# Turning a strided copy out of PSUM around, and shifting attention steps by one slot, in a fused attention and gated feed-forward kernel

## Chip, cores, metric

One core of one Trainium2 chip. The metric is device time in microseconds (us); every kernel was run several times and medians are quoted. One run of each is profiled, and its "span" (first to last instruction) is 1 to 2 us shorter than the time. Engines are named as in the profile: PE is TensorE (PEld its weight loads), ACT is ScalarE, DVE is VectorE, POOL is GpSimd, SP is SyncE. One scrambling of q and k by the copy, applied to the reference, moves its output by under 1%. The output check is a weak test of this copy; that the changed copy puts every element in its place is read from the code.

## The reference

```
q, k, v: 4 batches x 8 heads x 768 positions x 64, float32
k_sum = max of k over blocks of 32;  v_sum = mean of v over blocks of 32
scores = [ q k^T/8 where |i-j| < 16 ,  q k_sum^T/8 + log 32 ]
attn   = softmax(scores) [v ; v_sum]                       # x: 3072 x 512
out    = x + sigmoid(x w_res) * ((gelu(x w_gate) * (x w_val)) w_out)   # d_ff = 1536
```

## The kernel before

The work is cut into eight units: half a batch each, 384 rows of x. The code fixes the order of the instructions on each engine. A unit has a stage A (twelve steps of gate and value matmuls, gelu, product) and a stage B (six output steps, two per 128 rows). Work for later units is hung into slots: in stage A the transposes of the next batch's k (even units) or q (odd units), in stage B the next unit's attention. Six of the eight units carry transposes; unit 6 has attention work but no transposes; unit 7 has neither.

```python
def transpose_pair(src, dst, pad, hp, pool, tag, copy):     # hp: pair of heads
    tp = pool.tile([128, PJ, PP], BF16, ...)                # PSUM, PJ = 8, PP = 96
    for j in range(PJ):
        for hh in range(2):
            nc.tensor.transpose(tp[hh*64:hh*64+64, j, :], src[:, 2*hp+hh, j, :], ident[0:PP, 0:PP])
    o = dst[:, pad:pad + S].rearrange("d (p j) -> d j p", j=PJ)   # position = 8 p + j
    if copy == "act":
        nc.scalar.copy(o, tp[:])
    else:
        nc.vector.tensor_copy(o, tp[:])
```

```python
# stage A: slots in the feed-forward loop
at(("A", 3 * hp + 1), lambda hp=hp: k_step(nb, hp, ps_t, "t"))      # even units; q_step in odd ones
# stage B: slots in the output loop
for hp in range(NP):
    at(("B", hp), lambda hp=hp: s_step(u + 1, hp, nst))             # scores, exp, mask -> P
    at(("B", hp + 1), lambda hp=hp: av_step(u + 1, hp, nst))        # P v -> xn
at(("B", 4), lambda: xt_step(u + 1, 0, nst, ps_t, "t"))             # transpose of xn -> xT
at(("B", 5), lambda: xt_step(u + 1, 1, nst, ps_t, "t"))
for fo in range(FO):
    fo_step(st, gvT, fo)            # g, vv: 8 matmuls; gelu on ACT; product on DVE
    for fn in slots.get(("A", fo), []): fn()
for i in range(2 * NSUB):
    for fn in slots.get(("B", i), []): fn()
    out_step(u, st, gvT, i // 2, i % 2)   # even: r, f(0-3), tanh; odd: f(4-11), th and o on DVE
```

The softmax here doesn't subtract the row's maximum and nothing guards it: scores larger than these inputs give would overflow.

Of the kernel before, what the change touches and what calls it, by code (L numbers as in the profile page):

```python
# [15 lines left out]
def kernel(  # L16
# [11 lines left out]
    nc = tc.nc  # L28
    B, H, S, D = q.shape
# [13 lines left out]
    NSUB = TU // 128  # L43
# [4 lines left out]
    PJ = 8  # L48
# [11 lines left out]
    ps_t = ctx.enter_context(tc.tile_pool(name="ps_t", bufs=1, space=bass.MemoryType.PSUM))  # L60
# [17 lines left out]
    def load_qk(src, b, parts, name):  # L78
        t = qk.tile([PP, H, PJ, D], BF16, tag=name, name=name)
        hs = H // parts  # L80
        for i in range(parts):
            nc.gpsimd.dma_start(
                out=t[:, i * hs:(i + 1) * hs].rearrange("p h j d -> p h (j d)"),
                in_=src[b, i * hs:(i + 1) * hs].rearrange("h (p j) d -> p h (j d)", j=PJ),
            )
        return t
# [9 lines left out]
    with tc.manual_schedule():  # L96
# [66 lines left out]
        def transpose_pair(src, dst, pad, hp, pool, tag, copy):  # L163
            tp = pool.tile([128, PJ, PP], BF16, tag=tag, name="tp")
            for j in range(PJ):
                for hh in range(2):
                    nc.tensor.transpose(tp[hh * 64:hh * 64 + 64, j, :], src[:, 2 * hp + hh, j, :],  # L167
                                        ident[0:PP, 0:PP])
            o = dst[:, pad:pad + S].rearrange("d (p j) -> d j p", j=PJ)
            if copy == "act":  # L170
                nc.scalar.copy(o, tp[:])  # L171
            else:
                nc.vector.tensor_copy(o, tp[:])

        def k_step(b, hp, pool, tag, copy="act"):
            transpose_pair(k_sb[b], kT[b % 2][hp], WIN, hp, pool, tag, copy)
# [20 lines left out]
        def s_step(u, hp, st):  # L197
            b, half = u // 2, u % 2
            s = ps_s.tile([128, 2, 512], F32, tag="s", name="s")
            kt, qt = kT[b % 2][hp], qT[b % 2][hp]  # L200
            for t in range(HT):
                tt = half * HT + t
                for hh in range(2):
                    ps = slice(hh * 64, hh * 64 + 64)
                    nc.tensor.matmul(s[:, hh, t * QT:(t + 1) * QT], kt[ps, tt * QT:tt * QT + 128],
                                     qt[ps, tt * QT:(tt + 1) * QT], start=True, stop=True,
                                     skip_group_check=True)
            for hh in range(2):
                ps = slice(hh * 64, hh * 64 + 64)
                nc.tensor.matmul(s[96:128, hh, 0:TU], ksum[b % 2][hp][ps, :],  # L210
                                 qt[ps, half * TU:(half + 1) * TU], start=True, stop=True,
                                 skip_group_check=True)
            P = work.tile([128, 2, HT, QT], BF16, tag="P", name="P")
            nc.scalar.activation(P.rearrange("p a t q -> p a (t q)"), s[:, :, 0:TU], AF.Exp,  # L214
                                 scale=scale, bias=bias_t[:])
            Pf = P.rearrange("p a t q -> p (a t) q")
            nc.vector.tensor_mul(Pf, Pf, maskt.unsqueeze(1).to_broadcast([128, 2 * HT, QT]))  # L217
            st["P", hp] = P

        def av_step(u, hp, st):  # L220
            b, half = u // 2, u % 2
            P = st["P", hp]
            ao = ps_o.tile([128, NSUB, 2, D + 1], F32, tag="ao", name="ao")
            for sub in range(NSUB):
                for hh in range(2):
                    for e in range(2):
                        t = 2 * sub + e
                        nc.tensor.matmul(ao[64 * e:64 * e + 64, sub, hh, :], P[:, hh, t, :],  # L228
                                         vext[b % 2][:, half * HT + t, 2 * hp + hh, :],
                                         start=True, stop=True, skip_group_check=True)  # L230
            rz = work.tile([128, NSUB, 2, 1], F32, tag="rz", name="rz")
            nc.vector.reciprocal(rz[:], ao[:, :, :, D:D + 1])
            xn = st["xn"].rearrange("p s (h d) -> p s h d", d=D)[:, :, 2 * hp:2 * hp + 2, :]
            nc.vector.tensor_mul(xn, ao[:, :, :, 0:D], rz.to_broadcast([128, NSUB, 2, D]))  # L234

        def xt_step(u, g, st, pool, tag):
            xp = pool.tile([128, 2, TU], BF16, tag=tag, name="xp")
            for i in range(2):
                ko = 2 * g + i
                for sub in range(NSUB):  # L240
                    nc.tensor.transpose(xp[:, i, sub * 128:(sub + 1) * 128],
                                        st["xn"][:, sub, ko * 128:(ko + 1) * 128], ident[:])
            nc.vector.tensor_copy(st["xT"][:, 2 * g:2 * g + 2, :], xp[:])
# [20 lines left out]
        def out_step(u, st, gvT, sub, part):  # L264
            ss = slice(sub * 128, (sub + 1) * 128)
            if part == 0:
                r = ps_mm.tile([128, 512], F32, tag="mm", name="r")
                for ko in range(KO):
                    nc.tensor.matmul(r[:], st["xT"][:, ko, ss], w_res[:, ko, :],  # L269
                                     start=(ko == 0), stop=(ko == KO - 1))  # L270
                th = work.tile([128, DM], F32, tag="th", name="th")
                nc.scalar.activation(th[:], r[:], AF.Tanh, scale=0.5)  # L272
                f = ps_mm.tile([128, 512], F32, tag="mm", name="f")
                for fo in range(4):
                    nc.tensor.matmul(f[:], gvT[:, fo, ss], w_out[:, fo, :],  # L275
                                     start=(fo == 0), stop=False)
                st["f"], st["th"] = f, th
            else:
                f, th = st["f"], st["th"]
                for fo in range(4, FO):  # L280
                    nc.tensor.matmul(f[:], gvT[:, fo, ss], w_out[:, fo, :],  # L281
                                     start=False, stop=(fo == FO - 1))
                nc.vector.scalar_tensor_tensor(th[:], th[:], 1.0, f[:], ALU.add, ALU.mult)  # L283
                o = work.tile([128, DM], F32, tag="o", name="o")
                nc.vector.scalar_tensor_tensor(o[:], th[:], 0.5, st["xn"][:, sub, :], ALU.mult, ALU.add)
                row = u * TU + sub * 128
                nc.sync.dma_start(out=out[row:row + 128, :], in_=o[:])
# [30 lines left out]
        for u in range(NU):  # L318
            b, half = u // 2, u % 2
            nb = b + 1  # L320
            if half == 0 and nb < B:
                k_sb[nb] = load_qk(k, nb, 1, "k_sb")
                q_sb[nb] = load_qk(q, nb, 1, "q_sb")
                v_loads(nb)
            slots = {}

            def at(key, fn):
                slots.setdefault(key, []).append(fn)

            if nb < B:  # L330
                for hp in range(NP):
                    if half == 0:
                        at(("A", 3 * hp + 1), lambda hp=hp: k_step(nb, hp, ps_t, "t"))
                    else:
                        at(("A", 3 * hp + 1), lambda hp=hp: q_step(nb, hp, ps_t, "t"))
                if half == 1:
                    at(("A", 6), lambda: vsum_mm(nb, ps_t, "t"))
                    at(("A", 6), lambda: vsum_bc(nb, 0, 4, nc.gpsimd))
                    at(("A", 6), lambda: vsum_bc(nb, 4, 8, nc.gpsimd))
                    at(("A", 6), lambda: vsum_bc(nb, 8, NT, nc.gpsimd))  # L340
            nst = None
            if u + 1 < NU:
                nst = new_unit()
                for hp in range(NP):
                    at(("B", hp), lambda hp=hp: s_step(u + 1, hp, nst))
                    at(("B", hp + 1), lambda hp=hp: av_step(u + 1, hp, nst))
                at(("B", 4), lambda: xt_step(u + 1, 0, nst, ps_t, "t"))
                at(("B", 5), lambda: xt_step(u + 1, 1, nst, ps_t, "t"))
            gvT = upool.tile([128, FO, TU], BF16, tag="gvT", name="gvT")
            for fo in range(FO):  # L350
                fo_step(st, gvT, fo)
                for fn in slots.get(("A", fo), []):
                    fn()
            for i in range(2 * NSUB):
                for fn in slots.get(("B", i), []):
                    fn()
                out_step(u, st, gvT, i // 2, i % 2)
            st = nst


# [28 lines left out]
```

## Time and profile before

| | before |
|---|---|
| time | 383.67 us (382.7 to 385.25, 3 runs) |
| span of the profiled run | 381.9 us |
| first g matmul | 54.1 us |
| units with transposes (six) | 42.1 to 45.8 us each |
| unit 6, no transposes | 31.4 us |
| unit 7, no next unit | 30.8 us |

The first line of the page has each engine's busy time, with its share of the span and its number of instructions:

```profile
PE 295.3 (77%) x2640; PEld 155.7 (41%) x2640; DVE 166.1 (44%) x324; ACT 212.1 (56%) x202; POOL 70.9 (19%) x88
```

No engine is full, so averages do not name the bottleneck. Cutting the span at the first g of each unit does. This is the view of busy time by window: start:end, length, then busy us and instructions of each engine, granted TensorE clock, DMA share, GB/s.

```profile
99.93:144.50 44.57, 37.81 (x337) 19.48 (x336) 17.21 (x33) 27.04 (x25) 16.13 (x17) 0.96 1.15 80
144.50:186.60 42.10, 34.10 (x325) 17.94 (x324) 19.87 (x36) 27.01 (x25) 0.00 (x0) 1.00 0.05 20
319.67:351.09 31.42, 30.88 (x262) 16.72 (x261) 16.71 (x32) 13.73 (x21) 0.00 (x0) 1.00 0.07 26
...
```

These are unit 1 (with q), unit 2 (with k) and unit 6 (no transposes). ACT is busy 27 us against 13.7. Four copies make that difference, as the groups by line and form show (the column before the bar is the count; after it busy us and mean ns of one):

```profile
L171 ACT COPY kT_1_94<-tp 128x768 bf16<-128x768 bf16 x2 | 7.2, 3578 | 2.2 <-PE tp L167 2.2
L173 DVE COPY qT_3_100<-tp 128x768 bf16<-128x768 bf16 x1 | 3.6, 3557 | 0.0
L214 ACT ACTIVATE P<-s,bias_t 128x768 bf16<-128x768 f32 x32 | 28.8, 900 | 45.0 <-PE s L210 44.9
```

A copy of 128x768 takes four times as long as an exp of 128x768. What that does at the end of stage A is in the timeline of unit 1 (start, duration, instruction; in brackets the idle time before it and its releaser):

```profile
123.36 3.58 ACT L171 COPY qT_3_104<-tp 128x768 bf16<-128x768 bf16 x1 [0.62 <-PE tp L167]
...
126.44 0.83 ACT L261 ACTIVATE ge<-g 128x384 f32<-128x384 f32 x1
127.28 1.28 ACT L214 ACT_TABLE_LOAD   x1
...
128.58 0.90 ACT L214 ACTIVATE P<-s,bias_t 128x768 bf16<-128x768 f32 x1
...
129.51 0.56 DVE L217 TENSOR_TENSOR P<-P,maskt 128x768 bf16<-128x768 bf16 x1 [1.66 <-ACT P L214]
...
130.12 0.38 PE L228 MATMUL ao<-vext_114,P 128*64 128x65 bf16 x12 [3.02 <-DVE P L217]
...
130.99 3.11 PE L281 MATMUL f<-w_out,gvT 128*128 128x512 bf16 x8
```

Copy, delayed last gelu, table load, exp, mask, and PE idle for 3.02 us. After it the eight f matmuls need 3.11 us in place of 1.9: the clock had been halved for most of them (the mean granted clock from 130.99 to 134.03 is 0.59; in unit 0, whose eight f matmuls take 3.59 us, it is 0.50). The waits (who waited for whom: us in total, times, longest) give the totals:

```profile
PE ao L228 <- DVE P L217: 18.4, 7, 3.0
PE g L254 <- ACT ge L261: 18.0, 14, 1.3
```

### The profile page before, as it was taken

To read this page: it belongs to the slowest core of one execution; us is meant where nothing else is said; L and a number is where in the kernel's file an instruction comes from. 1 tells how busy PE (TensorE), PEld (TensorE's weight loads), DVE (VectorE), ACT (ScalarE), POOL (GpSimd) and SP (SyncE) were. 2 spreads that over 40 slices of the span, in tenths; PEclk is the share of its full clock that TensorE was granted. 3 is DMA by queue.
4 is the path that set the end of the run, shared out by engine and by line. 5 is a ranking of instruction groups with operands and counts; after the bars stand their busy time and mean duration, and the time that the engine had idled before them with its cause. 6 is when DMAs were issued, how large, how long until landed. Compare 5 with 4: busy or idle time off the path is not lost.

```text
span 381.9 us, 6251 instructions
## 1 busy us (share of the span) xinstructions
PE 295.3 (77%) x2640; PEld 155.7 (41%) x2640; DVE 166.1 (44%) x324; ACT 212.1 (56%) x202; POOL 70.9 (19%) x88
## 2 busy tenths in 40 slices
PE   0421668669978698878978698777988699999995
PEld 0320244334544244434544344433554345645652
DVE  4044863434522264335523263435622256456432
ACT  0699317773476745785485736685376833353420
POOL 8523364000008530000007530000004100000000
PEclk9999969987999899999999899998999989999999
DMA  8999999900100991000100994000100001000002
GB/s 156 205 193 197 200 152 121 23 0 30 57 0 6 189 130 47 2 1 29 57 0 2 177 130 64 0 3 8 50 27 2 0 29 57 0 21 36 29 1 82
DMA packets 54843, 23.95 MB, mean 63 GB/s; under 512 B 37408, under 2 KB 51744, under 8 KB 54816
## 3 DMA queue, kind: packets, MB, share of 16 engines
q0 software_dynamic: 42208, 14.98, 51.6%
q1 hardware_dynamic: 8032, 7.44, 6.9%
q10 hardware_dynamic: 4576, 1.15, 1.4%
q8 instruction: 20, 0.33, 0.4%
q14 instruction: 7, 0.06, 0.0%
HBM read 32.24 MB, written 6.29 MB: 101 GB/s over the span
## 4 chain that ended last, share of the span: by engine, by line
PE 49%; ACT 24%; issue 13%; DVE 10%; ACTq 2%; DMA 1%; DVEq 0%
PE f L281 13%; PE vv L258 10%; PE g L254 8%; PE vs L188 3%; PE tp L167 3%; ACT ge L261 3%; PE r L269 2%; PE ao L228 2%; ACT L214 2%; ACTq L105 2%; PE f L275 2%; DVE P L217 2%; ACT kT_1_94 L171 2%; ACT kT_0_93 L171 2%; ACT qT_1_102 L171 2%
## 5 line engine op out<-in xcount | busy, mean ns | idle before, releaser
L254 PE MATMUL g<-xT,w_gate 128*128 128x384 bf16 x384 | 79.0, 328 | 19.3 <-ACT ge L261 18.0
L261 ACT ACTIVATE ge<-g 128x384 f32<-128x384 f32 x96 | 53.0, 573 | 60.9 <-PE g L254 46.3
L262 DVE TENSOR_TENSOR gvT<-ge,vv 128x384 bf16<-128x384 f32 x96 | 51.4, 551 | 78.3 <-ACT ge L261 45.3
L258 PE MATMUL vv<-xT,w_val 128*128 128x384 bf16 x384 | 78.6, 328 | 2.9 <-DVE gvT L262 2.9
L254 PEld LDWEIGHTS <-w_gate 128*128 128x128 bf16 x384 | 35.4, 98 | 47.2 <-issue 24.7
L214 ACT ACTIVATE P<-s,bias_t 128x768 bf16<-128x768 f32 x32 | 28.8, 900 | 45.0 <-PE s L210 44.9
L281 PE MATMUL f<-w_out,gvT 128*128 128x512 bf16 x192 | 52.4, 422 | 0.0
L258 PEld LDWEIGHTS <-w_val 128*128 128x128 bf16 x384 | 37.7, 98 | 29.7 <-issue 5.6
L195 POOL COPY vext_114<-vsum_116 32x2048 bf16<-32x2048 bf16 x6 | 11.1, 1894 | 117.0 <-DVE vsum_116 L190 117.0
L217 DVE TENSOR_TENSOR P<-P,maskt 128x768 bf16<-128x768 bf16 x32 | 20.1, 632 | 20.6 <-ACT P L214 20.5
L281 PEld LDWEIGHTS <-gvT 128*128 128x128 bf16 x192 | 18.8, 106 | 24.8 <-issue 10.3
L283 DVE SCALAR_TENSOR_TENSOR th<-th,f 128x512 f32<-128x512 f32 x24 | 16.5, 688 | 27.2 <-PE f L281 27.2
L272 ACT ACTIVATE th<-r 128x512 f32<-128x512 f32 x24 | 14.3, 594 | 25.0 <-PE r L269 24.6
L228 PEld LDWEIGHTS <-P 128*64 128x64 bf16 x384 | 9.5, 118 | 39.0 <-DVE P L217 28.9
L269 PE MATMUL r<-w_res,xT 128*128 128x512 bf16 x96 | 24.8, 381 | 0.0
L275 PE MATMUL f<-w_out,gvT 128*128 128x512 bf16 x96 | 24.6, 379 | 0.0
L195 POOL COPY vext_113<-vsum_115 32x2048 bf16<-32x2048 bf16 (+1 forms) x4 | 9.1, 2303 | 74.4 <-DVE vsum_115 L190 74.4
L292 POOL DMA_DIRECT2D vext_114<-in_v_dram x24 | 18.2, 761 | 12.9 <-DMA k_sb<-in_k_dram 5.9
L167 PE MATMUL tp<-ident,k_sb 96*64 96x96 bf16 x256 | 9.8, 227 | 12.2 <-DMA k_sb<-in_k_dram 9.6
L228 PE MATMUL ao<-vext_113,P 128*64 128x65 bf16 x192 | 6.9, 214 | 15.0 <-DVE P L217 9.0
L234 DVE TENSOR_TENSOR xn<-ao,rz 128x384 bf16<-128x384 f32 x32 | 17.8, 558 | 1.1
L167 PE MATMUL tp<-ident,q_sb 96*64 96x96 bf16 x256 | 9.8, 227 | 10.0 <-DMA q_sb<-in_q_dram 4.9
(139 smaller groups left out, 338.4 us busy)
## 6 DMA issues: line engine op xcount, KB each, us to landing
out_dram<-o SPq DMA_DIRECT2D x24, 256.0 KB, 2.0
k_sb<-in_k_dram POOLq DMA_DIRECT2D x3, 768.0 KB, 7.5
q_sb<-in_q_dram POOLq DMA_DIRECT2D x3, 768.0 KB, 10.7
vext_114<-in_v_dram POOLq DMA_DIRECT2D x20, 96.0 KB, 10.5
w_gate<-in_moe_w_gate_dram POOLq DMA_DIRECT2D x6, 256.0 KB, 14.8
w_val<-in_moe_w_val_dram POOLq DMA_DIRECT2D x6, 256.0 KB, 14.5
w_out<-in_moe_w_out_dram POOLq DMA_DIRECT2D x3, 512.0 KB, 14.0
vst<-in_v_dram ACTq DMA_DIRECT2D x5, 192.0 KB, 11.1
```

What stands on the lines that cost most here:

```text
L167: nc.tensor.transpose(tp[hh * 64:hh * 64 + 64, j, :], src[:, 2 * hp + hh, j, :], ident[0:PP, 0:PP])
L171: nc.scalar.copy(o, tp[:])
L214: nc.scalar.activation(P.rearrange("p a t q -> p a (t q)"), s[:, :, 0:TU], AF.Exp, scale=scale, bias=bias_t[:])
L217: nc.vector.tensor_mul(Pf, Pf, maskt.unsqueeze(1).to_broadcast([128, 2 * HT, QT]))
L228: nc.tensor.matmul(ao[64 * e:64 * e + 64, sub, hh, :], P[:, hh, t, :], vext[b % 2][:, half * HT + t, 2 * hp + hh, :], start=True, stop=Tru ...
L254: nc.tensor.matmul(g[:, 0:TU], w_gate[:, ko, fs], st["xT"][:, ko, :], start=(ko == 0), stop=(ko == KO - 1))
L258: nc.tensor.matmul(vv[:, 0:TU], w_val[:, ko, fs], st["xT"][:, ko, :], start=(ko == 0), stop=(ko == KO - 1))
L261: nc.scalar.activation(ge[:], g[:, 0:TU], AF.Gelu)
L262: nc.vector.tensor_mul(gvT[:, fo, :], ge[:], vv[:, 0:TU])
L269: nc.tensor.matmul(r[:], st["xT"][:, ko, ss], w_res[:, ko, :], start=(ko == 0), stop=(ko == KO - 1))
L275: nc.tensor.matmul(f[:], gvT[:, fo, ss], w_out[:, fo, :], start=(fo == 0), stop=False)
L281: nc.tensor.matmul(f[:], gvT[:, fo, ss], w_out[:, fo, :], start=False, stop=(fo == FO - 1))
```

## The change

Intent: write SBUF contiguously and let the PSUM read be strided; and give the first scores of the next unit one more slot before they are used.

```diff
-            o = dst[:, pad:pad + S].rearrange("d (p j) -> d j p", j=PJ)
+            o = dst[:, pad:pad + S].rearrange("d (p j) -> d p j", j=PJ)
+            t_in = tp.rearrange("d j p -> d p j")
             if copy == "act":
-                nc.scalar.copy(o, tp[:])
+                nc.scalar.copy(o, t_in)
             else:
-                nc.vector.tensor_copy(o, tp[:])
+                nc.vector.tensor_copy(o, t_in)
@@ the attention slots of stage B
-                    at(("B", hp), lambda hp=hp: s_step(u + 1, hp, nst))
-                    at(("B", hp + 1), lambda hp=hp: av_step(u + 1, hp, nst))
-                at(("B", 4), lambda: xt_step(u + 1, 0, nst, ps_t, "t"))
-                at(("B", 5), lambda: xt_step(u + 1, 1, nst, ps_t, "t"))
+                    at(("B", hp + (hp > 0)), lambda hp=hp: s_step(u + 1, hp, nst))
+                    at(("B", hp + 2), lambda hp=hp: av_step(u + 1, hp, nst))
+                at(("B", 5), lambda: xt_step(u + 1, 0, nst, ps_t, "t"))
+                at(("B", 6), lambda: xt_step(u + 1, 1, nst, ps_t, "t"))
@@ after the output loop
+            for fn in slots.get(("B", 2 * NSUB), []):
+                fn()
```

So the first scores keep slot 0, and everything after them is one slot later; the last transposes of x come after the last output step.

## The prediction

> What bounds the kernel now. The timeline gives the starts of the eight half-batch units (first g matmul): 54.1, 99.9, 144.5, 186.6, 231.2, 275.0, 319.7, 351.1 us, end 381.9. The first six last 42 to 46 us; the seventh, the only one that overlaps next-unit attention but copies no transposes, lasts 31.4. The difference is ScalarE. The groups show each transpose copy (128x768 bf16 out of PSUM) at 3.58 us, 30 on ScalarE and 2 on VectorE; the exp over 128x768 takes 0.90. In the feed-forward loop three steps cost TensorE 3 x 1.30 us, but ScalarE 3 x 0.50 plus 3.58, so the gelus come late, g waits for them (18 us in the waits), and the last gelu of each loop delays table load, exp and mask: TensorE then idles 3.0 us before the first ao, and the granted clock falls to 0.5 afterwards in most of these units.
>
> Why the copy is slow: it writes 2-byte elements 16 bytes apart. [...] The change writes contiguously and reads PSUM at 192-byte steps. No instruction of this trace shows what a long strided PSUM read costs. I take 0.9 us, estimated from the exp of the same size; anything to about 1.9 us still hides behind the matmuls.
>
> Gains, on the critical path in the six copying units. Estimate from the seventh unit: 31.4 plus 4 transposes at 0.46 = 33.3 for a k unit; plus 2.8 for the vs matmuls = 36.1 for a q unit. Against 42 to 46 this saves 8 to 12 us per unit, about 57 in all.
>
> The prologue: copies and vext casts end at 41.5, vs at 43.8. With fast copies the casts would wait for the vst transfers, about 30 us by the DMA packets, so the first g could start near 42. But the next k load, issued behind the weights on a queue full until 48.5, should then land at 52 to 54, and the in-order TensorE would wait for it at the transposes of step 1 (57.9 before). So I expect 4 to 5 us gained, not 12, and a cold clock costing up to 3.
>
> Cost of the reordering. It removes the wait for the first P (0.5 us in the seventh unit). But the last xT copy now stands after the last th and o on VectorE (0.69 each), and the next g needs it: I expect TensorE to idle about 1.7 us at each of seven unit boundaries where there was none. Net +0.6 to +0.9 us per unit, 4 to 6 in all: the schedule change alone should lose slightly.
>
> Sum: unit 1 starts near 87 (99.9 before); then 37, 34, 37, 34, 37, 32.3, 30.8: span 329, time about 331 us, range 323 to 344. Faster 0.94, same 0.04, slower 0.02.
>
> What shows it: copies near 0.9 us on ScalarE; ScalarE busy from 212 to about 130 us; g waits on ge near zero; no 3 us wait before ao and no half clock there; unit periods 34 and 37; in unit 0 TensorE waiting for k_sb until 52 to 54; new waits of g for xT of about 1.7 us.
>
> What would make it wrong: a strided PSUM read as slow as the strided write (then within 2%); at 2 us half of the gain goes; the k load arriving earlier or later; VectorE slowed by GpSimd copies that now collide with it[...].

The "cold clock costing up to 3" was the estimate; what the runs show for it is a slow stretch after the wait for k_sb. From the transposes after that wait to the next ones it takes 6.08 us in the trace after (the following stretch takes 4.47), so 1.6 us are lost, and 7.44 in E4 against 4.47 in E6, so 3.0.

## The result and the profile after

333.95 us median (332.96 to 334.12, 3 runs) against 383.67. The ratio is 0.8692, with a 95% interval of 0.8639 to 0.8746. Ratios here are the mean time of one kernel's fast runs over that of the other's of the same rounds, so not quite the ratio of the medians quoted. The output is correct.

Engine totals, then the same three units by window (1, 2 and 6):

```profile
PE 284.7 (86%) x2640; PEld 153.8 (46%) x2640; DVE 162.4 (49%) x324; ACT 134.8 (41%) x202; POOL 71.1 (21%) x88
```

```profile
86.37:123.78 37.41, 35.98 (x339) 18.97 (x337) 17.30 (x34) 16.75 (x25) 15.46 (x17) 1.00 0.81 75
123.78:158.36 34.58, 33.15 (x328) 17.96 (x325) 20.15 (x37) 16.75 (x25) 0.67 (x1) 1.00 0.54 46
267.75:300.06 32.31, 30.88 (x264) 16.71 (x262) 16.62 (x33) 13.75 (x21) 0.00 (x0) 1.00 0.07 25
...
```

The copying units lost 7 to 9 us each (unit 0: 5.9), and the start 7.7 us (first g at 46.45). Units 6 and 7, which have no copies, became slower: 32.31 against 31.42, and 32.34 against 30.81. The sum of all differences is the 49.5 us between the spans. The groups name the copies:

```profile
L172 ACT COPY kT_1_94<-tp 128x768 bf16<-128x768 bf16 x2 | 1.6, 800 | 1.2 <-PE tp L167 1.2
L174 DVE COPY qT_3_100<-tp 128x768 bf16<-128x768 bf16 x1 | 0.9, 947 | 0.0
L215 ACT ACTIVATE P<-s,bias_t 128x768 bf16<-128x768 f32 x32 | 28.8, 901 | 46.0 <-PE s L211 45.9
```

3.58 us became 0.80 on ACT, 3.56 became 0.95 on DVE. In the waits of PE, g no longer waits for the gelu nor ao for P; new are these two:

```profile
PE tp L167 <- DMA k_sb<-in_k_dram: 13.9, 2, 9.3
PE g L255 <- DVE xT L244: 9.7, 7, 1.4
```

The second line is the price of the new order. The end of unit 0 on PE and DVE, in the timeline:

```profile
84.31 1.89 PE L282 MATMUL f<-w_out,gvT 128*128 128x512 bf16 x8
...
86.31 0.69 DVE L284 SCALAR_TENSOR_TENSOR th<-th,f 128x512 f32<-128x512 f32 x1 [0.92 <-PE f L282]
86.37 0.49 PE L255 MATMUL g<-xT,w_gate 128*128 128x384 bf16 x2
87.03 0.69 DVE L286 SCALAR_TENSOR_TENSOR o<-th,xn 128x512 f32<-128x512 f32 x1
87.64 0.55 DVE L244 COPY xT<-xp 128x768 bf16<-128x768 bf16 x1
88.25 0.48 PE L255 MATMUL g<-xT,w_gate 128*128 128x384 bf16 x2 [1.38 <-DVE xT L244]
```

DVE runs these in the order in which the code emits them: th at 86.31, o at 87.03, xT at 87.64. Since the last transposes of x are emitted after the last output step, their copy comes behind th and o and starts about 1.1 us after the transposes are done (they run from 86.04 to 86.54). PE runs the two g matmuls whose half of xT is ready, then waits 1.38 us; this happens at all seven unit boundaries.

The first line is new in its second wait (the first, 9.3 us, is the start of the kernel and was there before). PE reaches the first k transposes of the second batch too early:

```profile
48.96 0.81 PE L259 MATMUL vv<-xT,w_val 128*128 128x384 bf16 x4
54.41 0.85 PE L167 MATMUL tp<-ident,k_sb 96*64 96x96 bf16 x16 [4.64 <-DMA k_sb<-in_k_dram]
55.20 1.46 PE L255 MATMUL g<-xT,w_gate 128*128 128x384 bf16 x4
```

The g after it takes 1.46 us in place of 0.81: the half clock again (granted clock 0.50 from 55.20 to 56.66).

### The profile page after: what moved, and what is told of

Read it like the earlier page. It is cut to its first block, busy times and chain, and to the rows that moved or that the text cites. A ratio compares the mean times of both kernels' runs of the same rounds, so it can differ in the third digit from the quotient of the medians.

```text
span 332.4 us, 6258 instructions
## 1 busy us (share of the span) xinstructions
PE 284.7 (86%) x2640; PEld 153.8 (46%) x2640; DVE 162.4 (49%) x324; ACT 134.8 (41%) x202; POOL 71.1 (21%) x88
## 3 DMA queue, kind: packets, MB, share of 16 engines
q1 hardware_dynamic: 8032, 7.44, 8.0%
## 4 chain that ended last, share of the span: by engine, by line
PE 75%; DMA 10%; DVE 9%; SPq 2%; issue 1%; POOL 1%; ACT 0%; DVEq 0%; ACTq 0%
PE g L255 19%; PE vv L259 19%; PE f L282 13%; DMA vst<-in_v_dram 6%; PE r L270 5%; PE f L276 5%; DMA k_sb<-in_k_dram 4%; PE vs L189 4%; PE tp L167 3%; DVE th L284 3%; DVE o L286 3%; PE ao L229 2%; PE s L206 2%; SPq L105 2%; PE s L211 2%
## 5 line engine op out<-in xcount | busy, mean ns | idle before, releaser
L255 PE MATMUL g<-xT,w_gate 128*128 128x384 bf16 x384 | 80.8, 330 | 9.7 <-DVE xT L244 9.7
L263 DVE TENSOR_TENSOR gvT<-ge,vv 128x384 bf16<-128x384 f32 x96 | 53.1, 553 | 73.2 <-PE vv L259 73.2
L262 ACT ACTIVATE ge<-g 128x384 f32<-128x384 f32 x96 | 47.1, 491 | 96.2 <-PE g L255 63.0
L282 PE MATMUL f<-w_out,gvT 128*128 128x512 bf16 x192 | 45.4, 379 | 0.0
L282 PEld LDWEIGHTS <-gvT 128*128 128x128 bf16 x192 | 17.9, 98 | 20.6 <-issue 1.2
L276 PE MATMUL f<-w_out,gvT 128*128 128x512 bf16 x96 | 24.6, 379 | 0.0
L286 DVE SCALAR_TENSOR_TENSOR o<-th,xn 128x512 f32<-128x512 f32 x24 | 16.6, 692 | 0.8
L167 PEld LDWEIGHTS <-k_sb 96*64 96x64 bf16 x256 | 7.9, 127 | 17.8 <-DMA k_sb<-in_k_dram 14.3
## 6 DMA issues: line engine op xcount, KB each, us to landing
vst<-in_v_dram ACTq DMA_DIRECT2D x5, 192.0 KB, 11.4
```

What stands on the lines that cost most here:

```text
L167: nc.tensor.transpose(tp[hh * 64:hh * 64 + 64, j, :], src[:, 2 * hp + hh, j, :], ident[0:PP, 0:PP])
L255: nc.tensor.matmul(g[:, 0:TU], w_gate[:, ko, fs], st["xT"][:, ko, :], start=(ko == 0), stop=(ko == KO - 1))
L262: nc.scalar.activation(ge[:], g[:, 0:TU], AF.Gelu)
L263: nc.vector.tensor_mul(gvT[:, fo, :], ge[:], vv[:, 0:TU])
L276: nc.tensor.matmul(f[:], gvT[:, fo, ss], w_out[:, fo, :], start=(fo == 0), stop=False)
L282: nc.tensor.matmul(f[:], gvT[:, fo, ss], w_out[:, fo, :], start=False, stop=(fo == FO - 1))
```

## The experiments

My theory: the contiguous write gives all of the gain; the strided read is free; the new order costs about 1 us a unit through the xT queue; the start is now bound by the k load. Rivals: the order gives a real part of the gain, since it hides the wait for P; or the strided read still costs something. E1 to E4 ran on one chip (before there: 384.8 us), E5 to E8 on another (before there: 384.52 us).

### E1: the copy alone

Edit: the copy hunk of the change, not the slots.

> The changed copy with the old order of the attention steps. My theory (the copy gives all of the gain, the new order loses a little): about 4 to 6 us faster than both parts together, 328 to 330 us; TensorE waits 0.5 to 0.8 us for the first P of a unit, and no g waits for xT. Rival (the new order gives a real part, since it hides the wait for the first P that was 3 us before): slower than both parts together, 337 us or more.

Measured: 327.52 us (326.84 to 328.93, 5 runs), ratio 0.8518 (0.8491 to 0.8545). E3, both parts on the same chip, took 334.35. The copy alone is 6.8 us faster than both, and its time is just below my range of 328 to 330. The rival's 337 or more falls. No g waits for xT; the wait for P is smaller than I expected:

```profile
PE ao L229 <- DVE P L218: 2.5, 7, 0.4
PE xp L242 <- DVE xT L244: 1.3, 7, 0.2
```

### E2: the order alone

Edit: the slot hunks of the change, not the copy.

> The new order with the old, strided write of the copy. My theory: little to gain, 375 to 383 us; the wait before the first ao of a copying unit falls from 3.0 to about 1.4 us, the half-clock windows after it become fewer, and a wait of g for xT of about 1.4 us appears at seven unit boundaries and takes most of it back. Rival (the order gives a real part of the 50 us): 370 us or less.

Measured: 373.36 us (372.52 to 373.62, 4 runs), ratio 0.9697 (0.9668 to 0.9725). This is 11.4 us faster than before, outside my range and short of the rival's. The expected waits are there:

```profile
PE g L254 <- DVE xT L243: 9.7, 7, 1.4
PE ao L228 <- DVE P L217: 7.7, 6, 1.3
```

The xT wait costs 9.7 us and 10.7 us less are spent waiting for P (18.4 before), which nearly cancels. What I under-rated is the clock. Before, five of the six copying units show a mean granted clock of 0.90 or 0.96; in this run it is 1.00 over the whole span. In unit 1 the f matmuls around the wait now run at full speed:

```profile
124.90 1.89 PE L281 MATMUL f<-w_out,gvT 128*128 128x512 bf16 x8
128.07 0.38 PE L228 MATMUL ao<-vext,P 128*64 128x65 bf16 x12 [1.28 <-DVE P L217]
```

From the first scores of unit 2 (in unit 1's stage B) to the first vv of unit 2 this kernel takes 18.50 us; the kernel before took 20.51. The kernel before holds a control for this. In its unit 2 PE waits just as long for P, but the f matmuls after the wait run at full speed:

```profile
173.71 0.38 PE L228 MATMUL ao<-vext_114,P 128*64 128x65 bf16 x12 [3.01 <-DVE P L217]
174.57 1.90 PE L281 MATMUL f<-w_out,gvT 128*128 128x512 bf16 x8
```

With the new order unit 2 gains only 0.5 us (42.10 to 41.59, from first g to first g), while units 1, 3, 4 and 5, whose f matmuls had taken 2.92 to 3.54 us, gain 2.0 to 2.2. In unit 0 they had taken 3.59 us, so before, five of the six waits of 3.0 us were followed by slow f matmuls; after the wait of 1.28 us shown above the next four r matmuls take 1.04 us, as ahead of it. Why unit 2 differs from the other five, these runs do not show. So the sign of the order change depends on the copy: with slow copies it saves 11 us, mostly by keeping the clock up, which is an inference from these two traces, with unit 2 as the control; with fast copies, where the wait it hides is 0.4 us and no half clock follows it, only its cost is left. The means of the clock alone would be weak evidence, since the profile's figure can miss a slow stretch: in the trace after it reads 1.00 from 30.64 to 35.94, where the twelve vs matmuls take 5.30 us, against 2.79 in unit 1 of the trace before.

### E3: both parts again

> The changed kernel once more, on the same chip as the two halves, for comparison: 334 us, unit periods 37.4 (q unit) and 34.6 (k unit), 1.38 us wait of g for xT at seven boundaries.

Measured: 334.35 us (333.14 to 334.84, 4 runs), ratio 0.8682. As expected; it stands for the changed kernel in comparisons with E1, E2 and E4.

### E4: half a slot

Edit, on top of E1 (old slot numbers kept):

```diff
-        def out_step(u, st, gvT, sub, part):
+        def out_step(u, st, gvT, sub, part, mid=()):
@@ even part: after r and tanh, before f(0-3)
+                for fn in mid:
+                    fn()
@@ odd part: after f(4-7), before f(8-11)
                 for fo in range(4, FO):
+                    if fo == 8:
+                        for fn in mid:
+                            fn()
@@ the loop: slot 0 is run ahead of its output step as before, slots 1 to 5 are handed in as mid
```

> The changed copy, with every next-unit attention step after the first scores put half an output step later than in the old order (not a whole one), so that the last xT copy still stands before the last th and o on VectorE. My theory: the wait for the first P goes (0.5 to 0.8 us a unit) and the wait of g for xT goes too (1.4 us and more a unit): 9 to 12 us below both parts together, 322 to 325 us. Rival (waits at the unit boundary are not what bounds it, other waits take their place): within 3 us of the better of the old and the new order.

Measured: 322.07 us (320.8 to 323.99, 6 runs), ratio 0.8368 (0.8339 to 0.8398): 12.3 us below both parts (E3) and 5.5 below the copy alone (E1). In this trace neither ao waits for P nor g for xT. The first scores of unit 0's stage B, their ao, and the next unit's first g and vv:

```profile
71.83 0.35 PE L206 MATMUL s<-qT,kT 64*128 64x64 bf16 x12
...
75.07 0.38 PE L229 MATMUL ao<-vext,P 128*64 128x65 bf16 x12
...
86.73 0.81 PE L255 MATMUL g<-xT,w_gate 128*128 128x384 bf16 x4
87.38 0.81 PE L259 MATMUL vv<-xT,w_val 128*128 128x384 bf16 x4
```

From the first scores in unit 0's stage B to the next unit's first vv it takes 15.55 us; with both parts 17.27 (first trace after), with the copy alone 16.38. Seven times 1.72 is 12.0, and seven times 0.89 is 6.2: the boundary accounts for 12.3 and nearly all of 6.8. The order change was the right idea taken too far: four f matmuls hide the first P, eight push xT behind th and o.

### E5: the xT copy ahead of th and o

Edit, on the changed kernel: the last slot is handed to the last output step and run before its two DVE instructions.

```diff
+                for fn in tail:          # the last transposes of x and their xT copy
+                    fn()
                 nc.vector.scalar_tensor_tensor(th[:], th[:], 1.0, f[:], ALU.add, ALU.mult)
```

> The changed kernel, with one thing moved: at each unit's end the last transposes of x and their xT copy are put ahead of the last th and o on VectorE. My theory (the new order loses because xT queues behind th and o, 1.4 us each): the wait of g for xT falls from 1.38 us to about 0.3, 1.0 to 1.4 us a unit, 7 to 10 us in all, so 324 to 327 us, level with or just below the copy alone. Rival (the new order loses somewhere else, in the middle of the output stage): less than 3 us gained.

Measured: 326.52 us (325.89 to 327.65, 4 runs), ratio 0.8496 (0.8459 to 0.8533), against 0.8682 for both parts in the other job. Only one queue position changed, and the wait fell as expected:

```profile
PE g L255 <- DVE xT L244: 2.3, 7, 0.3
```

About 7 us come back. The new order loses in the DVE queue at the unit's end, and not in the middle of the stage.

### E6: half a slot, and the second k load ahead of the last weights

Edit, on top of E4:

```diff
+        k_sb[1] = load_qk(k, 1, 1, "k_sb")
         nc.gpsimd.dma_start(out=w_res[:], in_=moe_w_res...)
@@ start of a unit
-                k_sb[nb] = load_qk(k, nb, 1, "k_sb")
+                if nb > 1:
+                    k_sb[nb] = load_qk(k, nb, 1, "k_sb")
```

> The half-slot kernel, with the load of the second batch's k issued before those of the last weights (w_res, w_out). My theory (once the copies are fast, the start of unit 0 is bound by the landing of that k load, behind the weights): TensorE's wait for k_sb of about 4 us near 50 us goes, nothing waits for w_out, and the time falls by 4 to 7 us, to 315 to 318 us. Rival (transfers as a whole bound the start): the wait moves to another tile (w_res, w_out or vst), and less than 2 us is gained.

Measured: 314.42 us (313.35 to 315.43, 6 runs), ratio 0.8176 (0.8143 to 0.8208). The ratio fell by 0.0192 from E4, 7.4 us of 384.5, a little more than the upper end of my range; the two ran on different chips, so part of that may be the chips'. E4's trace has the wait at the second k load:

```profile
53.59 0.85 PE L167 MATMUL tp<-ident,k_sb 96*64 96x96 bf16 x16 [3.25 <-DMA k_sb<-in_k_dram]
```

In E6 it is gone, and PE waits for neither w_res nor w_out:

```profile
48.62 0.53 PE L168 MATMUL tp<-ident,k_sb 96*64 96x96 bf16 x16
49.08 0.82 PE L256 MATMUL g<-xT,w_gate 128*128 128x384 bf16 x4
```

The spans differ by 7.9 us: 3.6 between the first g and these transposes (3.25 of it the wait), 3.0 from these transposes to the next ones (7.44 us in E4, where the four g matmuls after the wait take 1.46 us, the half clock, and 4.47 in E6, where they take 0.82), and 1.4 because the first g came earlier (44.27 against 45.69). This last part is not explained; the two traces of the changed kernel differ by 0.75 us there.

This version is correct and beats both kernels: 18% below before, 6% below the change.

### E7: the step of the write

Its output is wrong, which doesn't matter for the time. Edit, on the kernel before: the copy reads contiguously and writes with a step of 4, 8, 16 or 32 bytes for head pairs 0 to 3.

```diff
+            n = (2, 4, 8, 16)[hp]
-            o = dst[:, pad:pad + S].rearrange("d (p j) -> d j p", j=PJ)
+            o = dst[:, pad:pad + S].rearrange("d (p j) -> d j p", j=n)
+            t_in = tp.rearrange("d j p -> d (j p)").rearrange("d (j p) -> d j p", j=n)
```

> Wrong results on purpose. The old kernel's copy with contiguous PSUM reads; the write step depends on the head pair: 4, 8, 16 and 32 bytes between 2-byte elements (pairs 0, 1, 2, 3). My theory [...]: 4 and 8 bytes well below the 3.58 us of 16 bytes, 32 bytes the same as 16. Rival (any step other than one element costs the full price): all four at about 3.6 us.

The four copies of one unit, in the order of the pairs:

```profile
54.06 1.02 ACT L173 COPY kT<-tp 128x768 bf16<-128x768 bf16 x1 [0.62 <-PE tp L167]
58.53 1.87 ACT L173 COPY kT<-tp 128x768 bf16<-128x768 bf16 x1 [0.62 <-PE tp L167]
63.21 3.58 ACT L173 COPY kT<-tp 128x768 bf16<-128x768 bf16 x1 [0.84 <-PE tp L167]
69.60 3.41 ACT L173 COPY kT<-tp 128x768 bf16<-128x768 bf16 x1 [1.10 <-PE tp L167]
```

With 0.80 us for a contiguous write (E8), the steps of 2, 4, 8, 16 and 32 bytes cost 0.80, 1.02, 1.87, 3.58 and 3.41 us. From 4 to 16 bytes the time, less a fixed 0.16 us, doubles with the step, and then it stops growing. My reading, an estimate from these times alone, is a price for each move of the write to another 16-byte piece: (3.58 - 1.87) us over the 384 more such moves is 4.5 ns each. That, plus the 0.16 us that remain, gives 1.87 us at 8 bytes by construction and 1.02 at 4 bytes, as measured. For the contiguous write (96 moves) it would give 0.59 us, not the 0.80 measured: there something else sets the time, and these runs do not show what. DVE pays nearly the same: 1.84 us at 8 bytes and 3.38 at 32 in this run. The rival, that any step pays in full, falls; E8 reads through patterns of the same shape at 0.80 us, so the shape of the pattern is not the cause either. The run also tests the prediction's "to about 1.9 us still hides": after the copy of 1.87 us no g waits for the gelu, after that of 3.58 us one waits 1.28 us (at 67.16). The program took 355.62 us in one run, with half of its copies slow.

### E8: the step of the read

Its output is wrong, which doesn't matter for the time. Edit, on the kernel before: the copy writes contiguously and reads PSUM with a step of 2, 4, 8 or 16 bytes for pairs 0 to 3.

```diff
+            n = (1, 2, 4, 8)[hp]
+            o = dst[:, pad:pad + S].rearrange("d (j p) -> d j p", j=n)
+            t_in = tp.rearrange("d j p -> d (j p)").rearrange("d (p j) -> d j p", j=n)
```

> Wrong results on purpose. The copy with contiguous writes; the PSUM read step is 2 (contiguous), 4, 8 and 16 bytes for head pairs 0, 1, 2, 3. My theory (a strided read out of PSUM costs ScalarE nothing): all four at 0.80 us, as the 192-byte step of the changed kernel. Rival (the 192-byte read is slower than a contiguous one, and the changed copy still pays for it): the contiguous one below 0.75 us.

```profile
54.99 0.80 ACT L173 COPY kT<-tp 128x768 bf16<-128x768 bf16 x1 [5.54 <-PE tp L167]
61.26 0.80 ACT L173 COPY kT<-tp 128x768 bf16<-128x768 bf16 x1 [0.63 <-PE tp L167]
65.73 0.80 ACT L173 COPY kT<-tp 128x768 bf16<-128x768 bf16 x1 [0.62 <-PE tp L167]
70.20 0.80 ACT L173 COPY kT<-tp 128x768 bf16<-128x768 bf16 x1 [0.63 <-PE tp L167]
```

All four take 0.80 us, as the 192-byte step of the change does. The strided read costs nothing here, so a contiguous read would gain nothing more. DVE's two copies (steps of 4 and 16 bytes) took 0.94 and 0.95 us, with the 192-byte step 0.95; a contiguous read and write on DVE was not measured.

## Why the prediction was right, and where it was off

The time (331 predicted, 333.95 measured) and most of its parts held: unit 1 starts at 86.4 us (87 predicted), it and the next units take 37.4, 34.6, 37.4, 34.6, 37.4, 32.3 and 32.3 us (37, 34, 37, 34, 37, 32.3, 30.8 predicted). Point by point:

- **The bottleneck.** "The difference is ScalarE": E1 takes away nothing but the long copies and gains 57.3 us (384.8 to 327.5). That this equals the "about 57 in all" for the six units is chance. In its trace units 1 to 5 gain 42.8 us, where the estimate (to 36.1 and 33.3 us) gives 44.8; they take 36.5 and 33.7 us. Unit 0 gains only 2.9, where the same estimate gives 12.5, because of the wait for k_sb, and the start gains 9.1 (54.8 in all between the spans). The prediction had foreseen this wait and counted it in the start.
- **The copy.** 0.9 us assumed, 0.80 measured. The estimate was borrowed from the exp of the same size (900 ns before, 901 after); the copy takes 800 ns. What makes up the 100 ns, these runs do not show. ACT busy fell to 134.8 us (130 predicted).
- **The start.** "The first g could start near 42" was too early: 46.45. The wait of the casts for vst was foreseen at about 30 us; the last cast started at 30.93 and ended at 31.35. What was left out is the work behind it: vs ended 4.6 us after the last cast, at 35.94, where it had been 2.3 us before (41.5 to 43.8), since its twelve matmuls took 5.30 us (2.79 at full speed, in unit 1 before). It did not matter for the total, because, as predicted, PE then waited for k_sb: until 54.4 us (52 to 54 predicted), with a half clock after it (0.50). E6 shows that this load was the bound.
- **The order.** The wait of g for xT was predicted at 1.7 us and is 1.38 at each boundary; the net loss was predicted at 4 to 6 us and is 6.8 (E3 less E1). The miss of 3.3 us in the span (329 to 332.4) is here: unit 7 takes 32.3 us, not 30.8, because it begins with that wait too, and I had charged the wait to units 1 to 6 only (1.5 us); units 1 to 5 are 0.4 to 0.6 us longer each (2.4 together), and unit 1 started 0.6 earlier.
- **One sentence was wrong as it stands**: "the schedule change alone should lose slightly". With the old copies it gains 11.4 us (E2). It holds only after the copies are fast. I had reckoned the waits, and not the half clock that followed five of the six 3.0 us waits (eight f matmuls 2.92 to 3.59 us, 1.90 in unit 2).
- **One risk named did not come.** "VectorE slowed by GpSimd copies" is not seen more than before: the one long mask multiply in the start takes 2.90 us beside a GpSimd copy of 3.53, and took 2.98 before (0.55 us elsewhere).

## What to carry to other kernels

In a rearranging copy like this one (bf16, ScalarE), let the strided side be the PSUM read and the contiguous side the SBUF write (0.80 us against 3.58 here, for 128x768), and test the read's cost with one run that sweeps the step. Measure the two halves of a change apart, and in both settings: whether a reordering helps depends on the wait it hides, and when another edit has removed that wait only its price remains. At a pipeline's seam look at the in-order queue of the engine that makes the next stage's operand (here DVE, whose xT copy behind th and o made PE wait 1.38 us); with the fast copy, half a slot gained 5.5 us over the old order here, where a whole one cost 6.8.
